# Another order for the early tasks and loads of a retention plus feed-forward kernel

## The chip, the cores and the metric

The kernel runs on one core of one Trainium2 chip. The metric is the device time of one execution in microseconds (us). The runs of the kernel before gave a median of 215.36 us (six runs, 214.33 to 216.28).

## What is computed

```python
# retention: q, k, v are [4 batches, 8 heads, 768 steps, 64]
gamma = 1.0 - 2.0 ** (-5.0 - np.arange(H))
for t in range(S):
    state = gamma * state + np.einsum('bhd,bhe->bhde', k[:, :, t], v[:, :, t])
    y[:, :, t] = D ** -0.5 * np.einsum('bhd,bhde->bhe', q[:, :, t], state)
# heads side by side: x is [4, 768, 512]; then norm, two matmuls and the residual
xn = (x - mean(x)) / np.sqrt(var(x) + 1e-6) * g_ln
out = x + np.maximum(xn @ w_ch1, 0.0) @ w_ch2          # 512 -> 2048 -> 512
```

## The kernel before

**Tiles.** The 3072 rows are cut into 24 tiles of 128 steps. Tiles 0 to 3 are the first chunks of the four batches, which need no state; tiles 4 to 8 are the further chunks of batch 0, and so on. The weights w1 (512 x 2048) and w2 (2048 x 512) are each loaded in four quarters, called w1_0 to w1_3 and w2_0 to w2_3. All loads come as f32 from HBM and are cast to bf16 on the way; GpSimd (POOL) issues them one after another (L430 for q, k, v, 256 KB of f32 each; L438 for a quarter of w, 1 MB of f32). Only k and q of tile 0 go through the queues of SyncE and ScalarE (L401).

**One early tile** (0 to 7) is this chain. The short names are used in the whole document; the tile's number follows them.

| name | engine, line | what it does |
|---|---|---|
| tk, tq | PE, L498, L505 | transpose k and q into PSUM banks b0 or b1 |
| ek, eq | ACT L256, DVE L510 | move k^T out; move q^T out times the decay qsc |
| pa, am | PE L538, DVE L562 | scores of 8 heads; times the decay mask |
| py | PE L586 | scores times v into bank b2 (of tiles 4 to 7 with the state's part, L582) |
| bn, xn, xc | DVE L601 and L602, DVE L613, ACT L619 | mean and variance; centred times g; x itself, kept for the residual |
| tx, ex | PE L672, ACT L256 | transpose of xn; its move out (xnt) |
| m1 g.h, re g.h | PE L719, ACT L732 or DVE L734 | first matmul of tile g for quarter h of w1 (16 matmuls of 128 columns); the relu of its result |
| vg, pd, pb | POOL L633, PE L645, DVE L659 | v times the decay; k^T vg into the state; its move out |
| m2 | PE, L757 | second matmul, 16 of 512 columns a tile; it needs all four quarters of w2 |

m1's result has two PSUM buffers (mm), so an m1 waits for the relu two before it. Tiles 8 to 23 are transposed by DMA (L520) and computed in groups of two and four.

**What sets the order.** All work is a list of 866 numbered tasks (`plan.add`). `ORDER` is that list written out by hand or by a search: the tasks are issued in exactly this order, each to the queue of its engine, so that every engine runs its own tasks in the order in which they stand there, and one that waits holds back all behind it. The hundreds of thousands of a number choose the bank (100186 is task 186 in b1), the ten thousands the engine. `Plan.order` runs through the list with assumed durations and gives each task an assumed start. With the order given, these starts are used in one place: `Plan.fill` (called in the last lines with `FILL` 0.8 and `FILL_END` 14000) puts matmuls on zeros (L785) in front of PE tasks for which the assumed start leaves PE idle, for 0.8 of that gap. It stops at the first task that takes the buffer `pd`:

```python
if t["takes"] and t["takes"][0] == "pd":
    end = 0
if t["eng"] == eng and t["start"] < end:
```

`w_pad` (`W_PAD`, L451) is a time that the planner adds to the assumed landing of a quarter of w. It reaches the program only through these fills.

**Start of the order before, by engine** (the lists are the tasks of the lines of ORDER that the diff touches):

- POOL: two index tables, v0, k1, q1, v1, **w1_0**, k2, q2, **w1_1**, v2, k3, q3, v3, **w1_2**, memset of the two state buffers (L341), vg0, k4, q4, v4, k5, q5, v5, **w1_3**, **w2_0**, k6, q6, k7, q7, v6, **w2_1**, vg4, vg5, **w2_3**, **w2_2**, k8, v8, q8, v7
- PE: tk0, tq0, pa0, gb (the row g spread to 128 partitions, L364), tk1, tq1, py0, pa1, tx0, py1, tk2, m1 0.0, tq2, pd0, tx1, pa2, m1 1.0, m1 0.1, py2, tk3, m1 1.1, tq3, tx2, pa3, m1 2.0, m1 2.1, py3, tk4, m1 0.2, tq4, m1 1.2, tx3, m1 2.2, pa4, tk5, ...
- ACT: ek0, gb's move out, ek1, gch (five small activations, L337), xc0, ex0, ek2, re 0.0, xc1, ex1, re 1.0, re 0.1, ek3, re 1.1, xc2, ex2, re 2.0, re 2.1, ek4, ...
- DVE: ..., eq0, am0, eq1, bn0, xn0, am1, bn1, xn1, eq2, pb4 (the state after pd0), am2, bn2, xn2, eq3, am3, ...

Of the kernel before, what the change touches and what calls it, by code (L numbers as in the profile page):

```python
# [21 lines left out]
    "bufs": {"qsb": 6, "ksb": 5, "vsb": 9, "qk": 8, "tr": 6, "vg": 3, "trq": 3, "trk": 3},  # L22
    "load_pad": 600, "w_pad": 1500, "lead": 32, "lead2": 32, "sq_at": 28000, "late_load": 1700, "two": 4, "m2b": ("b0",), "m2all": 16, "inter": 4, "every": 4, "tail": (0, 384, 512), "step": 8, "pace": 8, "ahead": 3,
    "slack": 600, "tr_pad": 4000, "x_pad": 3500, "vg_pad": 2500, "fill": 0.8, "fill_end": 14000,
}

ORDER = [int(x) for x in """
# [791 lines left out]
```

## Time and profile before

| what | value |
|---|---|
| profiled execution, its own time | 214.33 us |
| its span, first to last instruction | 212.6 us (so 1.73 us lie around it) |
| median of the six runs | 215.36 us |
| PE busy | 204.2 us, 96% of the span |
| DVE, POOL, ACT busy | 119.5, 96.8, 86.2 us |
| chain that ended last | PE 88%, DMA 3%, POOL 3% |
| queue of the loads that POOL issues | 77024 packets, 13.37 MB |

The busy time of PE is a modelled one, since matmuls overlap; the waits in front of its instructions are read from the view of waits and from the timeline. The landing of a load is the time from its issue to its last byte, and the list of DMA issues gives it for each, when it is asked for the few tenths of a us in which one load was issued.

| load | issued at us | landed at us | | load | issued at us | landed at us |
|---|---|---|---|---|---|---|
| v1 | 4.11 | 8.98 | | v3 | 10.80 | 19.62 |
| w1_0 | 4.97 | 11.92 | | w1_2 | 12.21 | 22.10 |
| k2 | 5.71 | 12.76 | | k4 | 14.89 | 23.05 |
| q2 | 6.59 | 13.61 | | q4 | 15.84 | 24.01 |
| w1_1 | 7.45 | 16.17 | | q5 | 18.69 | 26.63 |
| v2 | 8.19 | 17.12 | | v5 | 19.66 | 27.17 |
| k3 | 9.07 | 18.06 | | w1_3 | 20.52 | 29.74 |
| q3 | 9.93 | 19.36 | | w2_2 | 32.93 | 45.00 |

### The profile page before, as it was taken

The numbers are of one execution on the slowest core, as the hardware profiler recorded it, in microseconds if no ns is written. First come the engines' busy times: TensorE is split into PE (matmuls) and PEld (weight loads), VectorE is DVE, ScalarE is ACT, GpSimd is POOL, SyncE is SP. The second block draws the span as 40 slices with busy tenths as digits, with TensorE's granted clock in tenths as the row PEclk, the third lists the DMA queues.
The fourth block names the chain that finished last, engine by engine and source line by source line (L and its number), as shares of the span: only waits on it lengthen the run. The fifth ranks groups of instructions, "written<-read, shape, count | busy, mean of one in ns | idle before, by whom it ended". The sixth has DMA issues, their size and how long they took to land.

```text
span 212.6 us, 4939 instructions
## 1 busy us (share of the span) xinstructions
PE 204.2 (96%) x2005; PEld 130.6 (61%) x2027; DVE 119.5 (56%) x260; ACT 86.2 (41%) x175; POOL 96.8 (46%) x151
## 2 busy tenths in 40 slices
PE   7978999999999999999999999999999999999994
PEld 3457989985667666666676676574445444444442
DVE  5777766863675874763684777478686510030041
ACT  5456677660421323432343442261366601444200
POOL 8999697239778574846556739321000000000000
PEclk9999999999999999999999999999999999999999
DMA  9999999999999999999999999957442230010025
GB/s 130 171 180 180 164 197 175 208 126 125 109 114 122 144 132 212 152 122 215 139 169 160 105 185 137 103 123 94 83 158 67 76 123 5 0 49 0 0 87 212
DMA packets 108890, 26.85 MB, mean 126 GB/s; under 512 B 101569, under 2 KB 105921, under 8 KB 108866
## 3 DMA queue, kind: packets, MB, share of 16 engines
q0 software_dynamic: 77024, 13.37, 81.3%
q1 hardware_dynamic: 30642, 12.82, 28.1%
q10 hardware_dynamic: 1200, 0.33, 0.7%
q8 instruction: 16, 0.26, 0.5%
q14 instruction: 8, 0.07, 0.1%
HBM read 27.30 MB, written 6.29 MB: 158 GB/s over the span
## 4 chain that ended last, share of the span: by engine, by line
PE 88%; DMA 3%; POOL 3%; ACT 2%; issue 1%; DVE 1%; POOLq 0%; DVEq 0%
PE b L757 39%; PE mm L719 39%; DMA w<-in_moe_w_ch_dram 3%; PE pd L645 2%; PE pa L538 2%; PE b L572 2%; PE b L548 2%; POOL v L430 1%; PE b L672 1%; ACT L694 1%; PE b L586 1%; ACT xnt L256 1%; POOL vg L633 0%; PE b L498 0%; POOL state L341 0%
## 5 line engine op out<-in xcount | busy, mean ns | idle before, releaser
L719 PE MATMUL mm<-xnt,w 128*128 128x128 bf16 (+2 forms) x896 | 95.2, 257 | 0.8 <-ACT xnt L256 0.7
L757 PE MATMUL b<-w,h 128*128 128x512 bf16 (+2 forms) x379 | 88.4, 370 | 1.2 <-issue 0.2
L732 ACT ACTIVATE h<-mm 128x512 bf16<-128x512 f32 x93 | 55.0, 597 | 85.0 <-PE mm L719 84.7
L719 PEld LDWEIGHTS <-w 128*128 128x128 bf16 x896 | 66.1, 98 | 21.3 <-issue 0.9
L757 PEld LDWEIGHTS <-h 128*128 128x128 bf16 x400 | 37.0, 98 | 37.8
L562 DVE TENSOR_TENSOR asb<-pa,mask 128x1024 bf16<-128x1024 f32 x24 | 29.4, 1224 | 20.0 <-PE pa L538 19.7
L767 DVE SCALAR_TENSOR_TENSOR osb<-b,rstd,x_all 128x512 f32<-128x512 f32 (+2 forms) x25 | 18.0, 727 | 27.3 <-PE b L757 27.0
L601 DVE BATCH_NORM_STATS2 bns<-b 128x6 f32<-128x256 f32 (+1 forms) x40 | 17.8, 478 | 17.3 <-PE b L572 11.0
L619 ACT CAST x_all<-b 128x256 bf16<-128x256 f32 (+1 forms) x40 | 16.3, 417 | 22.6 <-DVE xn L613 21.3
L613 DVE SCALAR_TENSOR_TENSOR xn<-b,mv,gb 128x256 bf16<-128x256 f32 (+1 forms) x40 | 20.1, 532 | 0.8
L633 POOL TENSOR_TENSOR vg<-vsb,vsc 128x512 bf16<-128x512 bf16 x16 | 16.6, 1045 | 8.3 <-PE pd L645 7.8
L659 DVE TENSOR_TENSOR state<-pd,gch 64x256 bf16<-64x256 f32 x40 | 16.6, 414 | 4.3 <-PE pd L645 3.5
L430 POOL DMA_DIRECT2D vsb<-in_v_dram x20 | 18.1, 902 | 0.7 <-issue 0.6
L430 POOL DMA_DIRECT2D qk<-in_q_dram x16 | 14.2, 886 | 2.9 <-issue 2.4
L430 POOL DMA_DIRECT2D qk<-in_k_dram x16 | 14.3, 892 | 1.1 <-issue 1.1
L447 POOL COPY scrap<-qk 1x1 bf16<-1x1 bf16 x30 | 5.6, 186 | 16.3 <-DMA qk<-in_k_dram 9.3
L700 DVE RECIPROCAL rstd<-rstd 128x1 f32<-128x1 f32 (+2 forms) x14 | 2.0, 157 | 13.4 <-ACT rstd L694 13.4
L785 PE MATMUL pd<-zeros 128*128 128x512 bf16 (+1 forms) x24 | 6.6, 420 | 1.3 <-DVE zeros L291 1.2
L447 POOL COPY scrap<-vsb 1x1 bf16<-1x1 bf16 x15 | 2.7, 179 | 11.0 <-DMA vsb<-in_v_dram 11.0
L438 POOL DMA_DIRECT2D w<-in_moe_w_ch_dram x8 | 6.2, 774 | 2.7 <-DMA w<-in_moe_w_ch_dram 2.7
L572 PEld LDWEIGHTS <-asb 128*128 128x128 bf16 x128 | 5.8, 98 | 2.4
L430 POOL DMA_DIRECT2D qsb<-in_q_dram x7 | 6.3, 901 | 0.7 <-ACT trk L256 0.4
(68 smaller groups left out, 127.1 us busy)
## 6 DMA issues: line engine op xcount, KB each, us to landing
out_dram<-osb SPq DMA_DIRECT2D x23, 256.0 KB, 3.3
w<-in_moe_w_ch_dram POOLq DMA_DIRECT2D x8, 512.0 KB, 9.9
vsb<-in_v_dram POOLq DMA_DIRECT2D x20, 128.0 KB, 5.3
qk<-in_k_dram POOLq DMA_DIRECT2D x16, 128.0 KB, 4.6
qk<-in_q_dram POOLq DMA_DIRECT2D x16, 128.0 KB, 4.8
qsb<-in_q_dram POOLq DMA_DIRECT2D x7, 128.0 KB, 8.2
v<-in_v_dram POOLq DMA_DIRECT2D x4, 128.0 KB, 7.0
ksb<-in_k_dram POOLq DMA_DIRECT2D x4, 128.0 KB, 9.1
```

The source lines that it names most:

```text
L430: nc.gpsimd.dma_start(out=tile_of(kind, j), in_=src)
L562: nc.vector.tensor_tensor(out=take("asb", t, [P, NPAIR, 2, P], BF16).rearrange("p i a t -> p a i t"), in0=held["pa", t], in1=mask.rearrang ...
L572: nc.tensor.matmul(half_y[h % 2][:, h // 2 * D:(h // 2 + 1) * D], lhsT=held["asb", t][:, h // 2, h % 2, :], rhs=tile_of("v", t)[:, h, :], ...
L601: nc.vector.bn_stats(out=bns[:, t, i, :], in_=x)
L613: nc.vector.scalar_tensor_tensor(out=dst, in0=src, scalar=mv[:, t, 0:1], in1=g, op0=ALU.subtract, op1=ALU.mult)
L619: nc.scalar.copy(out=dst, in_=src)
L633: e.tensor_tensor(out=take("vg", j, [P, H, D], BF16), in0=tile_of("v", j), in1=vsc[:, cc, :].unsqueeze(2).to_broadcast([P, H, D]), op=ALU. ...
L659: nc.vector.tensor_tensor(out=held["pb", n][o, :, o], in0=held["pd", b][o, :, o], in1=gch[o, cc, :].unsqueeze(2).to_broadcast([D, NPAIR, D ...
L719: nc.tensor.matmul(p[:, j, :], lhsT=w1[:, ko, (ho + j) * P:(ho + j + 1) * P], rhs=held["xnt", hb][:, h0:h0 + n, ko, :], start=(ko == 0), s ...
L732: nc.scalar.activation(out=dst, in_=src, func=AF.Relu)
L757: nc.tensor.matmul(held[key][:, 0:w], lhsT=held["h1", hb][:, ho, i * P:(i + 1) * P], rhs=w2[:, ho, cols], start=(ho == 0), stop=(ho == HO ...
L767: nc.vector.scalar_tensor_tensor(out=take("osb", key, [P, w], FP32), in0=held[key][:, 0:w], scalar=rstd[:, t:t + 1], in1=x_all[:, t, cols] ...
```

## The change

One number of the planner and the first eight lines of ORDER; the same tasks stand in them before and after, and from `554 539 530` on nothing differs.

```diff
-    "load_pad": 600, "w_pad": 1500, "lead": 32, ...
+    "load_pad": 600, "w_pad": 550, "lead": 32, ...
 ORDER = [int(x) for x in """
-16 17 2 0 3 19 20 23 14 8 15 1 24 5 7 9 25 4 10 6 21 11 26 18 22 146 45 100147 149 148
-27 150 28 151 153 46 162 100163 29 152 154 164 165 30 155 12 166 31 156 167 32 157 158
-159 47 168 176 13 524 169 179 214 100177 170 525 33 215 178 171 172 216 180 34 173 181
-532 35 526 36 533 182 37 190 527 534 183 193 38 100191 184 535 48 192 185 186 194 187
-195 49 540 542 541 196 204 543 528 197 39 207 100205 198 536 529 40 200 42 43 41 206 544
-50 217 234 52 51 53 10537 55 208 100224 54 199 201 545 550 209 225 548 551 210 227 44
-226 251 202 549 552 228 218 56 211 546 553 547 222 275 212 219 538 229 235 220 100241
+16 17 2 0 3 19 20 23 14 8 15 1 24 5 7 9 25 4 10 6 21 11 26 18 13 22 146 100147 27 148 28
+29 149 30 45 150 151 162 46 31 100163 214 153 164 154 155 165 152 176 166 179 156 157
+100177 167 215 168 158 178 180 169 159 170 100190 172 32 33 171 173 193 524 181 47 525
+12 182 532 183 533 526 191 184 100186 527 534 192 216 187 194 540 535 185 195 542 196
+541 204 543 207 528 536 34 42 36 35 37 48 197 38 205 198 41 39 40 43 49 50 206 100200
+217 234 52 529 51 53 544 55 208 10537 224 201 54 545 199 550 209 100225 548 551 210 227
+44 226 251 202 549 552 228 218 56 211 546 553 547 222 275 212 219 538 229 235 220 100241
 554 539 530 10555 221 213 242 244 531 243 230 231 556 560 57 174 557 258 561 245 261 236
```

Read as names, the order after is:

- POOL: two index tables, v0, k1, q1, v1, **memset of the state**, k2, q2, v2, k3, **w1_0**, **w1_1**, q3, **vg0**, v3, k4, **w1_2**, q4, **k7**, k5, v4, q5, **w1_3**, v5, v6, k6, q6, q7, **w2_0**, **w2_1**, vg4, vg5, **w2_3**, **w2_2**, k8, v8, q8, v7
- PE: tk0, tq0, pa0, gb, tk1, tq1, py0, **tk2**, pa1, **tq2**, **pd0**, py1, tx0, **pa2**, **tk3**, tx1, **m1 0.0**, py2, m1 1.0, m1 0.1, tq3, tx2, m1 1.1, pa3, m1 2.0, m1 2.1, py3, tk4, m1 0.2, m1 1.2, tq4, tx3, m1 2.2, pa4, tk5, ... (and other banks for tq3, tx2, tk3, tq4, tx3, tk5, tq5)
- ACT: ek0, ek1, gb's move out, ek2, xc0, ex0, xc1, ex1, ek3, re 0.0, gch, re 1.0, re 0.1, ex2, re 1.1, xc2, re 2.0, re 2.1, ek4, ...; further on re 2.2 stands ahead of xc3 instead of behind it
- DVE: ..., eq0, am0, eq1, bn0, xn0, am1, **eq2**, bn1, xn1, am2, bn2, xn2, eq3, **pb4**, am3, ...

The queues of SyncE and ScalarE issue the same DMAs in the same order as before. No instruction is added or removed but for the fills, whose number follows from the planner's new starts.

More of the change, by code (lines that the diff above doesn't have):

```diff
@@ L22 @@
     "bufs": {"qsb": 6, "ksb": 5, "vsb": 9, "qk": 8, "tr": 6, "vg": 3, "trq": 3, "trk": 3},
-    "load_pad": 600, "w_pad": 1500, "lead": 32, "lead2": 32, "sq_at": 28000, "late_load": 1700, "two": 4, "m2b": ("b0",), "m2all": 16, "inter": 4, "every": 4, "tail": (0, 384, 512), "step": 8, "pace": 8, "ahead": 3,
+    "load_pad": 600, "w_pad": 550, "lead": 32, "lead2": 32, "sq_at": 28000, "late_load": 1700, "two": 4, "m2b": ("b0",), "m2all": 16, "inter": 4, "every": 4, "tail": (0, 384, 512), "step": 8, "pace": 8, "ahead": 3,
     "slack": 600, "tr_pad": 4000, "x_pad": 3500, "vg_pad": 2500, "fill": 0.8, "fill_end": 14000,
```

## The prediction

> **What bounds the kernel now.** I read the page first, then the waits of PE by stretches, then the timeline of the first 25 us, then the landings of the loads.
>
> ```profile
> span 212.6 us, 4939 instructions
> ...
> PE 204.2 (96%) x2005; PEld 130.6 (61%) x2027; DVE 119.5 (56%) x260; ACT 86.2 (41%) x175; POOL 96.8 (46%) x151
> ...
> PE   7978999999999999999999999999999999999994
> ...
> PEclk9999999999999999999999999999999999999999
> ```
>
> PE is the bound: full in every slice but the first four and the last. A change of early tasks can only earn what PE stands still early on. How much that is, is told by the waits of PE from 12 to 24 us:
>
> ```profile
> PE mm L719 <- ACT xnt L256: 0.7, 2, 0.4
> PE pd L645 <- POOL vg L633: 0.7, 1, 0.7
> PE b L672 <- DVE xn L613: 0.5, 1, 0.5
> PE b L498 <- DMA k<-in_k_dram: 0.3, 1, 0.3
> ```
>
> The same view from 24 to 46 us is empty. Since a matmul's modelled end covers part of a gap, I also took the gaps between starts: 0.44 (tk2 at 12.80), 0.86 (pd0 at 15.01), 0.53 (m1 1.0 at 16.29), 0.69 (tx2 at 20.34) and 0.56 us (m1 2.0 at 21.44), together **3.1 us**. Between py1 (12.12) and tk4 (23.45) PE has 8.3 us of work and these 3.1 us of waits. From tk4 on no gap reaches 0.36 us, and the only clear one up to 46 us is 0.29 us at 31.77. So I ask one question: **when can m1 0.2, the task after tk4, start?** In this execution it is 23.68 us. What is won there stays won, as far as no load is late afterwards.
>
> ```profile
> 4.97 0.79 POOL L438 DMA_DIRECT2D w<-in_moe_w_ch_dram  x1
> 12.21 0.76 POOL L438 DMA_DIRECT2D w<-in_moe_w_ch_dram  x1 [0.43 <-DMA w<-in_moe_w_ch_dram]
> 12.95 1.01 POOL L341 MEMSET state<- 128x512 bf16 x2
> 13.90 1.06 POOL L633 TENSOR_TENSOR vg<-v,vsc 128x512 bf16<-128x512 bf16 x1
> 15.01 0.38 PE L645 MATMUL pd<-vg,k 128*128 128x128 bf16 x4 [0.70 <-POOL vg L633]
> 23.43 0.24 PEld L498 LDWEIGHTS <-ksb 128*128 128x128 bf16 x4
> 23.68 1.06 PE L719 MATMUL mm<-xnt,w 128*128 128x128 bf16 x16
> ```
>
> These timeline lines show the first and third quarter of w1 being issued, the memset and vg0 behind them on POOL, pd0 waiting on vg0, and the task that I follow. The bracket at 12.21 is a rule of the load queue: w1_2 waited for w1_0 (landed 11.92), the load eight before it. All three such waits of POOL (2.7 us) fit this.
>
> **Part 1: the loads.** They land in the order of issue, one behind the other. Steps from one landing to the next: 2.94, 2.56, 2.48 us for w1_0, w1_1, w1_2; the six tiles between v1 and w1_2 share the rest, (22.10 - 8.98 - 7.98) / 6 = 0.86 us each. The new order gives k2 9.85, q2 10.7, v2 11.6, k3 12.4, w1_0 15.2, w1_1 17.8, q3 18.6, v3 19.5, k4 20.4, **w1_2 23.0** (what it was, plus k4 that now stands ahead), q4 23.9, k7 24.8, k5 25.7, v4 26.6, q5 27.4, w1_3 30.0. From w2_1 on the same bytes are ahead as before, so w2_2 keeps 45.0. Gains 2.9, 2.9, 5.5 and 5.7 us for k2, q2, v2, k3; losses 3.3 us (w1_0), 1.6 (w1_1), 0.9 (w1_2).
>
> Hole in the queue: k2 now stands behind the memset, issue at 4.97 + 1.0 = 5.97 (k2 before: 5.71, first w1_0 at 4.97). A load into an empty queue took 3.3 us (k9, issued at 46.14), which makes 9.3, ahead of its turn at 9.85; one into the loaded early queue took 4.9 us (v1), which makes 10.9. The bounds of the hole are 0 and 1.0 us; I take 0, since v1's 4.9 contain its turn behind q1.
>
> POOL's own wait moves: v6 is now eighth after w1_2 and is issued at 23.0 instead of about 21.4. Behind it stand k6, q6, q7, w2_0, w2_1, vg4 and vg5; k6 lands near 32.7 (33.17 before) for tk6 at 34.0. vg4 comes at 28.2 (28.95 before); vg5 waits for v5 (30.9) and ends at 32.0, pd5 took it at 33.56. Cost nothing; smallest cover 0.7 us, at pd5 shifted.
>
> **Part 2: the POOL queue up to vg0.** Before, vg0 starts at 13.90. Ahead of it v3 (0.87 from issue to issue), w1_2 (0.75) and the wait of 0.43 go away: 13.90 - 2.05 = 11.85, end 12.9. So pd0 comes at **13.0** instead of 15.01.
>
> **Part 3: PE up to m1 0.2.** Durations from rows (gap from start to start): transposes and pd 0.22, pa 0.33, py 0.23, m1 0.89 (16 x 56 ns); ACT 0.59 a move, 0.60 a relu, DVE eq 0.42, am 1.23, bn 0.88, xn 0.75.
> - tk2 9.9, pa1 10.1, am1 at 10.95 behind xn0 as before; tq2 10.75; PE is through at 11.0 and then stands for vg0, 2.0 us. py1, ready at 12.2, is held back by pd0: it comes at 13.2 instead of 12.12. That is the new wait.
> - pd0, py1, tx0, pa2, tk3: 13.0 to 14.25. bn1 and xn1 follow py1: 13.7 to 15.4. PE waits 1.2 us for tx1, 15.45.
> - m1 0.0 at 15.7 (xnt0 at 14.6, w1_0 15.2), py2 (am2 15.4 to 16.65) 16.6, m1 1.0 (xnt1 16.6) 16.8, m1 0.1 at 17.85 (w1_1 17.8; relu 0.0, behind ek3 on ACT, frees the buffer at 17.8; wait 0.2), tq3 18.75, tx2 19.0 (xn2 18.75), m1 1.1 19.2 (relu 1.0, behind gch, 19.0), pa3 20.1, m1 2.0 20.4 (xnt2 20.2), m1 2.1 21.3, py3 22.2 (am3 21.85), tk4 22.4, done 22.65.
> - Check: 13.0 + 8.0 of work + 1.4 of waits = 22.4 for tk4, against 23.45.
>
> Then m1 0.2 wants w1_2, which lands at 23.0: it starts at **23.05**, 0.63 earlier than 23.68. Without that wait it would be 22.65, 1.03 earlier.
>
> **Part 4: after it.** PE shifted by -0.63 meets q4 23.9 (tq4 now behind m1 1.2, 24.85), k5 25.7 (26.6), q5 27.4 (27.75, cover 0.3), v4 26.6 (py4 29.1), w1_3 30.0 (31.1), w2_2 45.0 (first m2 at 46.29 - 0.63 = 45.66, cover 0.66). None is late, so the 0.63 stays. The wait of 0.29 at 31.77 (ACT behind a table load of 1.28 at 29.65) shifts with the rest. Exchanged banks, the moved gch and xc3 have over 1 us of cover each: nothing. w_pad acts on fills alone; they stop at pd0, which now stands ahead of py1, so the fills before tx0 and py1 (8 matmuls at 10.21 and 11.23, all in gaps) go, some may come before tk2 and tq2 while these wait for their loads, and PE is bare from 11.0 to 13.0.
>
> **Two rules of the Trainium skill.** In the trace w1_0 lands at 11.92 and is used at 13.04. DMA: Bandwidth & Descriptors, section Rules for kernel authors, says to issue a DMA early and wait for it late; it speaks against moving w1_0 back, and by it alone m1 0.0 would lose 15.7 - 13.04 = 2.7 us. By the rows PE had waits enough behind it to take that in. The granted clock is 1.00 throughout the waits of 12 to 22 us. TensorE: Matmul & The Clock Gate, section Why this matters for your kernels, says that gaps up to some 3 us don't bring the clock down; the new 2.0 and 1.2 us would then be free.
>
> **Sum.** 214.33 - 0.63 = 213.7 us for a run like the profiled one, which was the fastest of the six. Against the median, 215.36 - 0.63 = **214.7 us**. About 0.5% (1.08 us) is what a measurement of this kernel can tell from no change.
>
> **Rivals.**
> - *More gain.* Landings were uneven by half a step (v3 came 0.26 after q3). If w1_2 lands by 22.6, PE isn't held: -1.03, 214.3; if tx1's wait is shorter as well, down to 213.8. For: the sum has PE ready at 22.65. Against: nothing else moves w1_2.
> - *No net gain.* The waits at pd0 and tx1 (3.2 us) replace the 3.1 removed and two small ones add up; or the orders are worth the same. 215.4.
> - *Slower: POOL late.* One queue carries memset, k2 and vg0; if it runs z later than summed (a longer memset, longer issues), py1 behind pd0 and the whole tile chain slip by z. From z = 1.03 the gain is gone; vg0 at its old end, 14.96, is z = 2.1: 24.75 at m1 0.2, +1.07, 216.4. For: pd0 is a fixed head of PE's queue. Against: the rows of issues differ by under 0.1 us each.
> - *Slower: the clock.* PE stands bare for 3.2 of the 4.4 us from 11.0. If the clock falls to the half pace of the start (nine fills in 3.38 us at 1.19, against four in 0.87 at 8.86), which lasted 4.7 us there, up to 2.3 us of dense work are lost: 22.65 + 2.3, +1.3, 216.6. For: PE was never this idle. Against: the clock held through 12 to 16 us, with 1.8 us of gaps. I take nothing.
>
> **Chances.** Forecast 0.52 (214.7; its own range 214.3 to 215.1), more gain 0.15, no net gain 0.11, POOL late 0.13, clock 0.09. Faster by over 0.5% (under 214.3): half of more gain and a tenth of the forecast, 0.13. Slower (over 216.4): half of the clock and half of POOL late, 0.11. Within: 0.76. The range 213.8 to 216.3 leaves out the ends of the clock and of POOL late.
>
> **What would show it.** Right: vg0 near 11.9, pd0 near 13.0, tx1 near 15.4 with a wait of about 1.2, w1_2 landing near 23.0 and m1 0.2 right behind it, an empty view of waits after that, PE's last matmul some 0.6 us earlier. Wrong: k2 landing after 10.5 (hole), a granted clock under 1.00 between 12 and 20 us, m1 0.2 after 23.5, or a wait of PE between 24 and 47 us on q5 or w2.

## The result, and the profile after

The kernel after takes a median of **216.56 us** (21 runs, 215.86 to 219.27); beside it the kernel before takes 215.03 us (47 runs). The ratio is 1.0079, with an interval of 1.006 to 1.0098: **slower**, where the forecast was 214.7 us, within 0.5%. The ratios, here and below, leave out the runs over 1.5% above the fastest of their kernel and are not those of the medians. The profiled execution took 217.47 us, 1.77 of them around its span.

The page of the kernel after: span, busy times, then two rows of the 40 slices (5.4 us each).

```profile
span 215.7 us, 4932 instructions
...
PE 205.1 (95%) x2001; PEld 132.3 (61%) x2022; DVE 119.4 (55%) x260; ACT 86.1 (40%) x175; POOL 97.0 (45%) x151
...
PE   7847999999999999999999999999999999999994
...
PEclk9995999999999999999999999999999999999999
```

Two things are new. The row of PE starts with 7847 where it was 7978: PE stands still more in the third slice. And PEclk, the clock that TensorE was granted, has a 5 in the fourth: it ran at half its clock there. From the fifth slice on both rows look as they did, and so the answer lies in the first 25 us. The waits of PE from 12 to 24 us (engine, operation, line, what it waited for; us in total, times, longest):

```profile
PE pd L645 <- POOL vg L633: 1.6, 1, 1.6
PE mm L719 <- DMA w<-in_moe_w_ch_dram: 1.5, 1, 1.5
PE b L672 <- DVE xn L613: 1.0, 1, 1.0
```

The first and the third line are the two waits that the forecast named, at pd0 and tx1. The second it had not: m1 0.0 waits for w1_0. The timeline of the kernel after (start, duration, engine, line, operation, number of instructions, and in brackets the wait before the first):

```profile
4.96 1.07 POOL L341 MEMSET state<- 128x512 bf16 x2
6.00 0.88 POOL L430 DMA_DIRECT2D k<-in_k_dram  x1
...
9.46 1.54 POOL L438 DMA_DIRECT2D w<-in_moe_w_ch_dram  x2
...
11.83 1.12 POOL L633 TENSOR_TENSOR vg<-v,vsc 128x512 bf16<-128x512 bf16 x1
...
13.00 0.38 PE L645 MATMUL pd<-vg,k 128*128 128x128 bf16 x4 [1.57 <-POOL vg L633]
...
15.49 0.54 PE L672 MATMUL b<-idn,xn 128*128 128x128 bf16 x4 [0.98 <-DVE xn L613]
...
17.50 1.89 PE L719 MATMUL mm<-xnt,w 128*128 128x128 bf16 x16 [1.47 <-DMA w<-in_moe_w_ch_dram]
19.62 3.28 PE L719 MATMUL mm<-xnt,w 128*128 128x128 bf16 x32
```

vg0, pd0 and tx1 stand within 0.05 us of the forecast. Then two things go wrong. m1 0.0 starts at 17.50, not 15.7, because w1_0 landed at 17.45, not 15.2. And its 16 matmuls take 1.89 us, where 16 of the same shape take 1.06 in the timeline of before: half the clock. The windows of PE show where that begins (stretch, its length, PE busy and instructions, granted clock, DMA share, GB/s):

```profile
8.77:12.19 3.42, 2.26 (x33) 1.00 1.98 127
12.19:15.60 3.41, 1.61 (x30) 1.00 1.11 149
15.60:19.01 3.41, 1.94 (x19) 0.50 1.44 186
19.01:22.42 3.41, 3.41 (x39) 0.50 1.89 179
22.42:25.84 3.42, 3.42 (x64) 1.00 2.04 169
```

From 15.60 to 22.42 us the granted clock is 0.50, right behind the stretch in which PE was busy for 1.61 of 3.41 us. In the second stretch at half pace PE is busy throughout: that is work that passes at half speed.

From m1 0.0 to m1 0.2 it took 9.26 us (17.50 to 26.76), 1.9 more than the forecast's 7.35. So m1 0.2 comes 1.8 + 1.9 = 3.7 us later than forecast, and 3.08 later than before (26.76 against 23.68). Not all of that is the clock's: w1_2, which m1 0.2 needs, landed at 25.13, so that at full clock it would still have come some 1.5 us later than before. By this estimate the loads have 1.5 of the 3.08 us and the clock 1.6. The last matmul of PE is 3.08 us later too (212.26 against 209.18). Nothing is lost or won back behind m1 0.2; the view of waits from 24 to 46 us is empty again.

### The profile page after: what moved, and what is told of

The parts are those of the page before. It is cut to its first block, busy times and chain, and to the rows that moved or that the text cites. A ratio compares the mean times of both kernels' runs of the same rounds, so it can differ in the third digit from the quotient of the medians.

```text
span 215.7 us, 4932 instructions
## 1 busy us (share of the span) xinstructions
PE 205.1 (95%) x2001; PEld 132.3 (61%) x2022; DVE 119.4 (55%) x260; ACT 86.1 (40%) x175; POOL 97.0 (45%) x151
## 4 chain that ended last, share of the span: by engine, by line
PE 88%; POOL 4%; DMA 4%; ACT 1%; issue 1%; DVE 0%; POOLq 0%
PE mm L719 40%; PE b L757 38%; DMA w<-in_moe_w_ch_dram 4%; PE pa L538 2%; PE pd L645 2%; PE b L572 2%; PE b L548 2%; POOL v L430 1%; POOL k L430 1%; POOL qsb L430 1%; PE b L586 1%; PE b L672 1%; ACT L694 1%; ACT h L732 1%; POOL state L341 0%
## 5 line engine op out<-in xcount | busy, mean ns | idle before, releaser
L719 PE MATMUL mm<-xnt,w 128*128 128x128 bf16 (+2 forms) x896 | 97.2, 262 | 1.6 <-DMA w<-in_moe_w_ch_dram 1.5
L719 PEld LDWEIGHTS <-w 128*128 128x128 bf16 x896 | 68.0, 100 | 22.2 <-DMA w<-in_moe_w_ch_dram 1.7
L256 ACT COPY xnt<-b 128x512 bf16<-128x512 bf16 x8 | 4.7, 585 | 5.1 <-PE b L672 5.1
L785 PE MATMUL pd<-zeros 128*128 128x512 bf16 (+1 forms) x20 | 5.5, 421 | 1.2 <-DVE zeros L291 1.2
L527 DVE TENSOR_TENSOR trq<-tr,qsc 128x512 bf16<-128x512 bf16 x16 | 6.5, 408 | 0.1
```

The source lines that it names most:

```text
L719: nc.tensor.matmul(p[:, j, :], lhsT=w1[:, ko, (ho + j) * P:(ho + j + 1) * P], rhs=held["xnt", hb][:, h0:h0 + n, ko, :], start=(ko == 0), s ...
```

## The experiments

**The theories.** *L, the loads:* the new order makes w1_0 land about 2 us late; within L, the memset in front of k2 (the hole in the queue), the small DMA that touches w1, or sharing with w1_1 could be the cause. *C, the clock:* PE is bare before m1 0.0, so that the clock falls. The rivals are one cause alone, or POOL and pd0. An execution is said to have lost the clock where its mean granted clock is under 0.995.

Each time is a median of 10 to 12 runs, beside 24 to 35 of the kernel before on the same chip. Edits are against the kernel after unless the text says before; `warm(ns)` is the planner's fill, `warm2(ns)` the same into a buffer of mm (a matmul of 512 columns on zeros for each 220 ns).

**e5: the kernel after once more,** with no edit, to see what varies between executions.

> The changed kernel unaltered, beside the three others on one chip. Both theories: slower than the kernel before by 0.6 to 1.0%. Theory clock and theory load in common: w1_0 lands 4 us or so behind k3, near 17; what differs between executions is the granted clock, so that a second profile need not show the half pace in the same place.

Measured 216.72 against 215.14 us, ratio 1.006 (1.0027 to 1.0094). Its profiled execution (215.57 us) kept the clock at 1.00, and so shows the new order with its late loads and without the fallen clock. Its timeline:

```profile
16.82 1.07 PE L719 MATMUL mm<-xnt,w 128*128 128x128 bf16 x16 [0.95 <-DMA w<-in_moe_w_ch_dram]
...
19.52 1.07 PE L719 MATMUL mm<-xnt,w 128*128 128x128 bf16 x16 [0.50 <-DMA w<-in_moe_w_ch_dram]
...
24.45 1.96 PE L719 MATMUL mm<-xnt,w 128*128 128x128 bf16 x32
```

The three lines are m1 0.0, 0.1 and 0.2. The first two wait for their quarters of w1 (landed 16.78 and 19.47); the third follows tk4 without a wait, its quarter having landed at 24.40. It comes 0.77 us later than before, and so does the last matmul, at 209.95: what the late loads cost in this execution, net of what the order gains. A size for the clock's part comes from executions of one kernel: in 14 of the 22 recorded executions of after the mean granted clock was under 0.995, with a median of 217.36 us; the other 8 have 216.24. That is 1.1 us, in nearly two of three executions. In e5 it was 8 of 12, 217.5 against 215.8. These are groups that formed by themselves, and they can differ in more than this fall: a clock that rises late at the start doesn't show in the mean (last section). Of the 128 executions of before that stand beside these experiments, one was under 0.995.

**e1: fills in the three waits,** loads left as they are.

```diff
+ e_pd, j == 0:            warm(1500)
+ e_tx, t == 1:            warm2(1000)
+ e_m1, key ("1", 0, 0):   warm2(1400)
```

> The changed kernel with matmuls on zeros in its three bare stretches of PE: 6 of 512 columns and 3 narrow ones ahead of pd0, 4 wide ones ahead of tx1, 6 ahead of m1 0.0; the loads are as in the changed kernel. Theory clock (the half pace from 15.60 to 22.42 us is the loss): granted clock 1.00 up to the last matmul, m1 0.2 near 25.2 instead of 26.8, the slow third of the times is gone, median 1.0 us or more under the changed kernel, near 215.5. Theory load (the first quarter of w1 lands at 17.45 and everything behind it comes 2 to 3 us late; the clock only adds to some runs): the clock is 1.00 as well, but m1 0.2 still waits for w1_2 near 25.1, and the median falls only to the level of the undisturbed runs of the changed kernel, 216.0 to 216.3, about 1 us over the kernel before.

215.91 against 215.48 us, 1.0008 (0.9977 to 1.004). The clock was under 0.995 in 2 of 12. w1_0 landed at 16.61. So the fills alone bring the kernel level with before, with w1_0 still late: C holds, as far as fills show it (e9 below has fills win something in the old order, too, where the clock had not fallen). The profiled execution was an odd one: 219.5 us, and the clock fell already at 7.52, ahead of all these fills.

**e7: bare PE in the kernel before.** Its fills end earlier; 12 of them, from 8.86 to 11.93 us, go.

```diff
-"fill_end": 14000
+"fill_end": 8800
```

> The kernel before without its fills from py0 on (12 to 13 matmuls on zeros at 8.86, 10.21 and 11.23 us, which lie in waits of PE); loads and order as before. Theory clock: PE now stands bare for about half of 8.9 to 16.0 us, the granted clock falls to half in part of the executions, the median rises by 0.5 us or more and single times reach 217 to 218. Theory load: loads as before, so the median stays within 0.3 us of the kernel before, as the order of work is untouched and no fill is on the path.

215.93 against 215.14 us, 1.0029 (0.9998 to 1.006). The clock fell in 10 of 12 executions; in the profiled one PE is busy 1.09 us between 9.00 and 12.40, and the clock is 0.50 from 12.40 to 15.80. So bare PE brings the clock down without the change's order. What it costs there isn't settled by an interval that holds 1. The two executions that kept the clock were even the slowest of the twelve (217.73 and 219.58 us), so the mean clock alone is no measure of the time.

**e2: the touching DMA** (L371, SyncE) moved from 2.2 to 7.7 us, behind a memset of its target.

```diff
-... 23 14 8 15 1 24 ... 100147 27 148 28
+... 23 14 8 1 24 ... 100147 27 148 15 28
+ tile 0, before it: nc.vector.memset(touch[:, 0, 0:1], 0.0)
```

> The changed kernel with the small DMA that reads 16 columns of each row of w1 (L371) issued near 6.8 us instead of 2.23, by a memset of one column of its target on DVE behind eq0. Theory touch (the packets of w1_0 are slow, up to 1.1 us each, because nothing has read these rows of w1 for some 5 us): w1_0 lands near 15.7 instead of 17.45, w1_2 near 23.4 instead of 25.13, m1 0.2 near 23.7, w2_2 near 45.1, median 215.2 or lower. Theory queue (w1_0 is slow because of what stands before and behind it in the queue, the touch plays no part): w1_0 stays near 17.4 and the median near 216.5.

216.72 against 215.48 us, 1.0044 (1.0014 to 1.0074); w1_0 at 17.15. The touch theory falls.

**e4: the kernel before without that DMA** (its 16 columns of w1 are then not touched ahead; nothing else reads them).

```diff
-lambda eng: nc.sync.dma_start(out=touch, in_=w1_v[:, :, 0:16])
+lambda eng: None
```

> The kernel before without the small DMA that reads 16 columns of each row of w1 at 2.23 us. The output is the same. Theory touch: the packets of w1_0 become slow as in the changed kernel, w1_0 lands 1.5 us later than its 11.92, all behind it too, median 1 us or more over the kernel before. Theory queue: w1_0 lands at 11.9 or some tenths sooner, median within 0.3 us of the kernel before.

216.21 against 215.48 us, 1.0026 (0.9997 to 1.0056), w1_0 at 12.37 instead of 11.92: unclear, and in any case no cause of the 5.5 us by which w1_0 lands later in after.

**e3: w1_0 ahead of the memset and of k2,** the rest as after.

```diff
-... 26 18 13 22 146 ... / 29 149 30 45 150 ...
+... 26 18 45 13 22 146 ... / 29 149 30 150 ...
```

> The changed kernel with only w1_0 back at its old place on POOL, ahead of the memset, k2, q2, v2 and k3; all else as changed. Theory load: w1_0 lands near 12 us as before the change, w1_2 near 22.5 to 23.0, no hole, first m2 as before; tiles 2 and 3 land near 13 to 16; PE stands for tk2 (12.8) instead of for vg0 and w1_0; median 215.0, at most 0.5 from the kernel before. Theory clock: PE stands bare for as long as in the changed kernel, the clock still falls in part of the runs, and the median stays over 216.

215.56 against 215.48 us, 1.0003 (0.997 to 1.0036). w1_0 lands at 12.37, but the tiles behind it come late (k2 13.31, k3 15.75), and m1 0.0 starts at 17.92 behind the tile chain. The place of w1_0 is a trade: what m1 0.0 no longer waits for, tk2 does (1.1 us).

**e8: e3 with fills** ahead of tk2 (900 ns) and tx1 (1000 ns).

```diff
 (e3)
+ e_tk, t == 2: warm(900)
+ e_tx, t == 1: warm2(1000)
```

> The changed kernel with w1_0 back at its old place (as in the run of that name) and matmuls on zeros in the waits ahead of tk2 and tx1. Theory clock: what the run with w1_0 back alone still lost in single executions goes; median 0.3 us or more under that run's, near 215.2 and not over the kernel before. Theory load: as the run without the fills, 215.5.

214.73 against 215.14 us, 0.9963 (0.9936 to 0.9989), the clock at full in all 12. In this second pair, e3 and e8, only the fills differ, and the ratio falls by 0.4%; the two ran on different chips and their intervals overlap, so it supports C without showing it.

**e6: the memset back behind q3,** right ahead of vg0, four tiles still ahead of w1_0.

```diff
-... 26 18 13 22 146 ... / ... 31 100163 214 153 ...
+... 26 18 22 146 ... / ... 31 100163 13 214 153 ...
```

> The changed kernel with only the memset of the state back behind q3, right ahead of vg0; the loads k2 to q3 are issued 1.0 us sooner. Theory hole (the memset ahead of k2 leaves the load queue short of work): k2, q2, v2, k3 land 0.5 to 0.9 us sooner (k3 near 12.4 instead of 13.1), w1_0 near 16.6 and w1_2 near 24.3, median about 0.7 us under the changed kernel. Rival: w1_0 is slow by itself, whatever is ahead; k3 sooner, but w1_0 and w1_2 within 0.3 of the changed kernel's 17.45 and 25.13, median within 0.3 us of it. Theory clock alone: the bare stretches are the same, so the median is the changed kernel's, too.

215.49 against 215.14 us, 1.0002 (0.9974 to 1.0031): 1.23 us under e5 on the same chip. k2 and k3 land at 10.23 and 12.78, about where they did (10.16 and 13.14), but w1_0 at 14.83 and w1_1 at 17.38; the expectation had it the other way round, more for the tiles and less for w1_0. The clock still fell in 8 of 12, at little cost here (median 215.49 against 215.32 in the other four). So L holds beside C, and its cause is the memset's place. The lists of DMA issues between 4.9 and 11.2 us (out, in, number, KB each, median us from issue to landing), first of after:

```profile
w<-in_moe_w_ch_dram POOLq DMA_DIRECT2D x2, 512.0 KB, 8.9
...
k<-in_k_dram POOLq DMA_DIRECT2D x2, 128.0 KB, 4.4
```

and of e6:

```profile
w<-in_moe_w_ch_dram POOLq DMA_DIRECT2D x2, 512.0 KB, 7.3
...
k<-in_k_dram POOLq DMA_DIRECT2D x2, 128.0 KB, 5.2
```

In after the tiles k2 and k3 spend 0.8 us less in the queue, since they were issued a memset later into a queue that moved on meanwhile; the quarters of w1 spend 1.6 us more, and are issued 1.0 us later on top of that (w1_0 at 9.46 against 8.43). The loss isn't at k2, where the forecast had looked for it, but at the first big load.

**e14: the memset between w1_0 and w1_1.** **e15: w1_1 behind q3,** with the memset still ahead of k2. Together they tell the memset from the sharing.

```diff
 e14
-... 26 18 13 22 146 ... / 29 149 30 45 150 ...
+... 26 18 22 146 ...    / 29 149 30 45 13 150 ...
 e15
-... 162 46 31 100163 214 ...
+... 162 31 46 100163 214 ...
```

> The changed kernel with the memset moved from ahead of k2 to between w1_0 and w1_1, so that w1_0 is issued near 8.4 and w1_1 where it was, near 10.2. Theory POOL time: w1_0 lands near 14.9, as in the runs with the memset behind q3, and the median falls by 0.5 us or more under the changed kernel. Rival (w1_0 shares the engines with the quarter issued right behind it): w1_0 also sooner, but because of the gap to w1_1; told apart by the next run.

> The changed kernel with w1_1 moved behind q3, so that no quarter is issued right behind w1_0; the memset stays ahead of k2. Theory POOL time: w1_0 stays late, at 16.5 or later, and the median stays within 0.4 us of the changed kernel. Rival (the two quarters share the engines): w1_0 lands near 15, q3 sooner by 2 us, median 0.4 us or more lower.

e14: 215.62 against 215.79 us, 0.997 (0.9939 to 1.0001), w1_0 at 14.94. e15: 217.29 against 215.79, 1.0065 (1.0029 to 1.01), w1_0 at 16.77. The sharing falls. Over the profiles of this order, w1_0 lands 3.2 to 4.3 us behind k3 where the memset stands ahead of k2 (after 4.31, e1 3.46, e2 3.81, e5 3.16, e10 3.98, e15 3.45) and 2.05 to 2.18 us where it doesn't (e6, e14, e11). The forecast had taken 2.8.

**e13: the memset ahead of w1_0 in the kernel before.**

```diff
-... 18 22 146 45 100147 ... / 159 47 168 176 13 524 ...
+... 18 22 146 13 45 100147 ... / 159 47 168 176 524 ...
```

> The kernel before with only the memset of the state moved ahead of w1_0, as the change has it. Theory POOL time (the 1.0 us of the memset delays the issue of the first quarter of w1, and a quarter that comes late finds the load engines at different points): w1_0 lands more than 1.0 us later than the 11.3 to 12.4 of the runs with the old order, at 13.3 or later, and w1_2 near 23.5 or later; vg0 comes 1 us sooner; median 0.3 us or more over the kernel before. Rival (what stands ahead in the queue, four tiles, makes w1_0 slow, not the memset): w1_0 at most 1.0 us later, near 12.8, w1_2 within 0.5 us of 22.1 to 22.8, median within 0.3 us.

215.83 against 215.79 us, 1.0004 (0.9974 to 1.0035), w1_0 at 12.00. So an early memset, and a w1_0 that is issued 0.94 us later (5.91 against 4.97), do no harm in themselves; they do with four tiles between. No run puts the memset between k3 and w1_0, which would tell the gap ahead of the tiles from the later issue of w1_0 behind them.

**e10: pd0 later,** behind tx0 (task 158), so that py1 doesn't stand behind vg0.

```diff
-100177 167 215 168 158 178 ...
+100177 167 168 158 215 178 ...
```

> The changed kernel with pd0 moved from ahead of py1 to behind tx0, so that PE no longer stands for vg0 with py1 behind it; the planner then also places 5 fills ahead of py1. Theory queue head (py1 behind pd0 behind vg0 is on the path): tx1 near 14.4 instead of 15.5 and m1 0.0 sooner by as much, median 0.5 us or more under the changed kernel's 216.6. Theory load: tx1 sooner, but m1 0.0 still starts when w1_0 lands, near 17, and the median stays within 0.4 us of the changed kernel, the fills taking part of the loss of clock.

217.93 against 215.56 us, 1.0084 (1.005 to 1.0118). The planner put five more fills ahead of py1, and the clock rose late in the profile, so that tx1 can't be compared; w1_0 landed at 17.02. What follows is only that moving pd0 doesn't mend the loss.

**e11: both mended,** e6's order and e1's first two fills. **e12: the same with w1_0 behind q2.** **e9: the kernel before with fills** in three of its waits.

```diff
 e11
 (e6)
+ e_pd, j == 0: warm(1500)
+ e_tx, t == 1: warm2(1000)
 e12
-... 26 18 13 22 146 ... 28 / 29 149 30 45 150 ... 31 100163 214 ...
+... 26 18 22 146 ... 28 / 45 29 149 30 150 ... 31 100163 13 214 ...
+ (the fills of e11)
 e9, against before
+ e_tk, t == 2: warm(400);  e_pd, j == 0: warm(700)
+ e_m1, key ("1", 1, 0): warm2(440)
```

> The changed kernel with the memset back behind q3 and with matmuls on zeros ahead of pd0 (1.5 us) and tx1 (0.9 us): loads without the memset ahead of them and a clock that holds. If these two, memset and bare stretches, are all that the sum on record had wrong, its gain comes out: m1 0.2 near 23.1 to 23.6 and a median 0.3 to 0.6 us under the kernel before. Theory load (w1_0 behind four tiles is slow by itself): w1_0 lands at 16.5 or later, w1_2 after 24, and the median is the kernel before's or above it.

> As the run with memset back and fills, with w1_0 moved up behind q2 (ahead of v2 and k3). Theory load: w1_0 lands near 13.3, v2 and k3 near 14.2 and 15.1, m1 0.0 near 15.7 with no wait for its weights, w1_2 near 23.0, m1 0.2 right behind it; median 0.6 us or more under the kernel before, the best of all. Theory clock alone: no better than the run with w1_0 ahead of k2 and fills, 0.4 us under the kernel before.

> The kernel before, order and loads untouched, with matmuls on zeros in three more of its own waits: 0.4 us ahead of tk2, 0.7 us ahead of pd0, 0.4 us ahead of m1 1.0. Theory clock (what w1_0 back at its place with fills won over the kernel before came from the clock): times draw together, median 0.3 us or more under the kernel before, near 214.7. Theory order (it came from the new order of tasks): no change of the median, within 0.2 us of the kernel before, or some tenths over, since the fills can run over.

All three on one chip, against 215.56 us. **e11: 214.50 us, 0.9936 (0.9911 to 0.9961);** e12: 214.45, 0.9948 (0.9918 to 0.9977); e9: 214.76, 0.9986 (0.9945 to 1.0027). e11 and e12 beat both kernels and can't be told apart. The timeline of e11:

```profile
8.43 1.56 POOL L438 DMA_DIRECT2D w<-in_moe_w_ch_dram  x2
...
10.78 1.09 POOL L341 MEMSET state<- 128x512 bf16 x2
11.73 1.14 POOL L633 TENSOR_TENSOR vg<-v,vsc 128x512 bf16<-128x512 bf16 x1
...
11.49 1.63 PE L789 MATMUL pd<-zeros 128*128 128x512 bf16 x9
...
14.53 1.03 PE L796 MATMUL mm<-zeros 128*128 128x512 bf16 x4
...
15.91 1.06 PE L723 MATMUL mm<-xnt,w 128*128 128x128 bf16 x16
```

Nine fills stand ahead of pd0 and four ahead of tx1, and m1 0.0 runs at full pace from 15.91, 0.2 from the forecast's 15.7. vg0 is no later than in after, although the memset now stands right ahead of it: POOL has the same sum of work either way. The view of waits of PE from 12 to 24 us has one line left:

```profile
PE b L505 <- DMA qsb<-in_q_dram: 0.5, 1, 0.5
```

It is tq3, for q3 (landed 19.48, forecast 18.6; 18.32 and 18.43 in e6 and e14). m1 0.2 starts at 23.55 and the last matmul at 209.05, before at 23.68 and 209.18: beside before's profiled execution, its fastest, the order with fills is 0.13 us ahead, not the forecast's 0.63. So of e11's gain of 1.06 us only a part is the order's: e9, the old order with fills, has a median 0.26 and a lowest time 0.40 us above e11's (214.76 and 214.45 against 214.50 and 214.05). Some 0.3 to 0.4 us are left for the order, if the medians are taken at their word, and the rest goes with the fills, perhaps by a clock that is steadier early, which no run isolates. e9's own interval holds 1, so that this split isn't settled.

## Why the prediction was wrong, point by point

- **What bounds the kernel: right.** PE from end to end; one question, when m1 0.2 starts; what is lost there stays lost (3.08 us at m1 0.2, 3.08 at the last matmul).
- **Part 2, POOL up to vg0: right,** vg0 at 11.83 and pd0 at 13.00. The rival "POOL late" didn't happen.
- **Part 3, the tile chain: right up to tx1,** py1 at 13.22 and tx1 at 15.49, with waits of 1.6 and 1.0 us. From m1 0.0 on it failed with the two steps below.
- **Part 1, the landings: the first step that failed,** "The bounds of the hole are 0 and 1.0 us; I take 0", with w1_0 at 15.2. The loads to k3 came within 0.75 us of their forecast, but w1_0 at 17.45 (16.6 to 17.15 in the other profiles of this order). The bounds were too narrow and set at the wrong load: its sign for the hole, k2 after 10.5, stayed away (10.16), and the hole came at w1_0. e6 and e14 show that the memset in front of k2 costs about 2 us there. Without it these landings would have held: w1_0 at 14.83 to 14.96 against 15.2 (the forecast's own steps add up to 15.35), and in e11 w1_2 at 22.92 against 23.0. The 3.3 us taken for a load into an empty queue were misread: when k9 was issued at 46.14, three loads issued before it were still to land (46.73 to 48.65). The steps behind w1_0 were right (w1_1 2.58 us later, w1_2 another 5.10), as was that PE waits for nothing after m1 0.2.
- **"From w2_1 on the same bytes are ahead as before, so w2_2 keeps 45.0": wrong with it.** It landed at 46.66 (45.62 in e5, 44.77 in e11): time in which the queue moved less isn't made up. PE, later still, met no wait there.
- **The clock, "I take nothing": the second step that failed.** The mechanism was written down as a rival, with 216.6 us and a chance of 0.09. It happened in 14 of 22 executions and lasted 6.8 us in the profiled one; the cost is 1.1 us by the executions, and some 1.6 us in the profiled one. The reason against it, that the clock had held through 12 to 16 us with 1.8 us of gaps, spoke for 1.8 idle of 4 us and not for 3.2 of 4.4. What told was the work in a step of 3.41 us, when the steps are counted from a profile's first clock record (changes of the clock stand whole steps apart). The emptiest early step of before, then one each of e5, e1 and e7:

```profile
12.64:16.06 3.42, 2.45 (x40) 1.00 1.66 186
12.38:15.79 3.41, 1.81 (x32) 1.00 1.22 176
4.10:7.52 3.42, 1.75 (x14) 1.00 2.23 142
9.00:12.40 3.40, 1.09 (x23) 1.00 1.81 180
```

  After has 1.61 and lost the clock; e1 and e7 lost it behind their lines. Before and e5 kept it. In the 17 profiles of this case, up to PE's last matmul, these three steps have the least work of PE, and no other is followed by a fall; the next are e5's 1.81 and one of 2.08 in e10. So the limit seems to lie near 1.8 of 3.41 us of PE's modelled busy time. Where the steps fall counts too: e5 is the same program as after, its steps begin 0.2 us later, and between 12.19 and 15.60 it had 1.62 and kept the clock. The forecast had counted 3.2 bare of 4.4 us and so had the number in hand.
- **The rule that the forecast weighed for the clock.** The Trainium skill, TensorE: Matmul & The Clock Gate, asks in "Why this matters for your kernels" for no idle gaps of PE over about 3 us between matmuls. No wait in after's early stretch is longer than 1.6 us, and the clock fell: the measurement decides, and the rule is too mild for stretches that are partly busy. The other, to issue early (DMA: Bandwidth & Descriptors, "Rules for kernel authors"), priced 2.7 us at m1 0.0; it lost 4.46 (13.04 to 17.50), of which the memset's place gave about 2.
- **The sum.** Against before's 215.03 the median rose by 1.53 us. The executions that kept the clock have a median 1.2 us above before's, the others 2.3 us. The late loads cost 0.77 us in e5's profile and by the estimate above 1.5 us in after's, so that the shares of the 1.53 us aren't settled; the two do not simply add up, either (in e6 the fall costs little). With either of the two taken away the kernel is level with before (e1 1.0008, e6 1.0002), without both it is faster (e11).
- **What stays open.** Why w1_0 is slow behind the memset. Between 8.8 and 10.6 us, w1's quarters just issued, the DMA moves 116 to 132 GB/s in the six profiles with the memset ahead of k2 and 149 to 153 in e6, e14 and e11. A queue of loads that has run nearly dry fits this, and the shorter 4.4 us of k2 and k3 too; but 30 GB/s over these 1.8 us are 54 KB, some 0.4 us of a transfer at 150 GB/s, not 2, and what slows w1_0's packets after that wasn't isolated. Open, too, are the exact limit of the clock, and what the order is worth by itself once both are mended.

## What to carry to other kernels

When an order of tasks gains time by letting an engine wait in one piece, add up how much the engine works in each stretch of the length in which the clock was seen to change (3.41 us here), not only how long the single gaps are, and put cheap fills into the wait. When an ordinary operation is moved ahead of loads on the queue that issues them, look for its price not at the next load alone but also at the big one behind it, where it stood here, and bound it by more than the operation's own duration. Two effects near the limit of what can be measured are best mended one by one and then together: here each alone only drew level (e1, e6), and both together beat the kernel before (e11). The old order with fills (e9) has to stand beside that before the gain is called the new order's.

## What the runs showed of the hardware that was not expected

- The moment at which the clock first rises varies from execution to execution: its first record lies between 4.0 us (e11) and 16.6 us (e13) in the profiles, though PE works from 1.2 us on. Before that record the matmuls run at half pace, and neither the mean clock nor the PEclk row shows it. In e13 the row is full of nines, and the spreading of g takes 2.07 us, where after and before have 1.12:

```profile
8.57 2.07 PE L364 MATMUL mm<-grow,ones 1*128 1x512 f32 x2
```

  From 6.35 to 16.59 us of e13 PE's modelled busy time fills three whole steps before the clock rises. The two profiles with the latest first record, e10 (15.98) and e13, belong to the longest times (218.92 and 218.87 us). This may well scatter the times of every kernel here, before's among them (214.33 to 217.82 us), but only one execution of each was profiled.
- All changes of the clock stand whole steps of 3.41 us apart (in after 5.36, 15.60, 22.42). Once down, it stayed down for 3.4 us in e7 and for 6.8 us in after and in e1; PE was busy throughout the last of these steps each time.
